# A^T W in three column parts, the first v chunk ahead of the weights, and softmax row sums as one more column of a product

## Chip, cores, metric

One core of one Trainium2 chip. The metric is the device time of one execution in microseconds (us). The span on a profile page is about 1.9 us shorter than the time of the same execution.

## The reference, cut to what matters

```python
# B, N, C = 4, 6144, 256; d_ff = 768; inputs float32
qn = q / (norm(q, axis=1) + 1e-6);  kn = k / (norm(k, axis=1) + 1e-6)
a = softmax(kn.transpose(0, 2, 1) @ qn / tau, -1)          # B x 256 x 256
x = (v @ a).reshape(B * N, C)
h = maximum(maximum(x @ w1, x @ w2), x @ w3)               # B*N x 768
out = h @ w_out                                            # B*N x 256
```

The kernel forms A^T W (`aw`, 256 x 768 for each of three weights) once per batch, and then runs 12 chunks of 512 rows of v through six h blocks each. It saves the product v A. The price is a short stage at each batch boundary: softmax, row sums, A^T W. Products land in tiles of PSUM; an eviction is the copy of such a tile to SBUF by ScalarE or VectorE, here with the scaling by 1/row sum, and frees the tile. The granted clock is the share of full speed that the profile shows for TensorE.

## The kernel before: what the change and the argument touch

```python
ps_h = tile_pool(name="ps_h", bufs=6, PSUM)   # h products, row sums and A^T W share six PSUM tiles
ps_x = tile_pool(name="ps_x", bufs=2, PSUM)
...
load_w(0)          # first halves (384 columns) of the three weights, software DMA queue
load_v(0)
load_w(1)          # second halves
load_v(1)
...                # w_out, load_v(2)

def rowsums(et):                                    # four one-column products
    ...
    DVE.reciprocal(out=rinv, in_=rs_ps[:, 0:CC])

def aw_half(et, rinv, aw, fh, at=(), between=None): # six groups: 3 weights x 2 row blocks
    for m in range(3):
        for ic in range(CC):
            ew = htile("ew_ps")
            for j in range(CC):
                PE.matmul(ew[:, :FH], lhsT=et[...], rhs=w_sb[m][:, j, fsl], ...)
            # evicted with scale=rinv, by ScalarE and VectorE in turn
...
def h_block(gi, aw, fc):                            # six products, then s_mx on ScalarE, two maxima on VectorE
    ...
et = softmax_t(*ps)
rinv = rowsums(et)
aw_half(et, rinv, aw, 0, [2], lambda: v_transpose_pe(0))  # v chunk 0 on TensorE
v_transpose(1)                                            # v chunk 1 by DMA transpose
for b in range(B):
    for ch in range(NCH):
        v_transpose(gi + 2)                               # DMA transpose, two chunks ahead
        if ch == 0:  gaps[0].append(lambda: aw_half(et, rinv, aw, 1))
        ...
        if more and ch == NCH - 1:                        # last chunk of a batch
            gaps[0]: norms; gaps[1]: exp_t; gaps[4]: rowsums
        for fc in range(FC):
            h_block(gi, aw, fc)
            for f in gaps[fc]: f()
        if more and ch == NCH - 1:
            aw_half(et, rinv, aw, 0)                      # behind the sixth h block
```

## Time and profile before

| | before |
|---|---|
| time, median | 586.5 us at first, 585.9 to 586.4 in the later sets |
| TensorE busy | 557.8 us, 95% of the span |
| TensorE waits for chunk 1's transpose | 5.0 us, once |
| twelve h products after that wait | 5.30 us (2.6 at the full clock), ending at 61.39 |
| first A^T W product to end of the second half, at a boundary | 5.30 us for 5.19 of work |

The prediction shows the lines of these. To read them: a wait counts only where it ends last.

### The profile page before, as it was taken

The numbers are of one execution on the slowest core, as the hardware profiler recorded it, in microseconds if no ns is written. First come the engines' busy times: TensorE is split into PE (matmuls) and PEld (weight loads), VectorE is DVE, ScalarE is ACT, GpSimd is POOL, SyncE is SP. The second block draws the span as 40 slices with busy tenths as digits, with TensorE's granted clock in tenths as the row PEclk, the third lists the DMA queues.
The fourth block names the chain that finished last, engine by engine and source line by source line (L and its number), as shares of the span: only waits on it lengthen the run. The fifth ranks groups of instructions, "written<-read, shape, count | busy, mean of one in ns | idle before, by whom it ended". The sixth has DMA issues, their size and how long they took to land.

```text
span 584.5 us, 9286 instructions
## 1 busy us (share of the span) xinstructions
PE 557.8 (95%) x3316; PEld 327.9 (56%) x3316; DVE 405.5 (69%) x623; ACT 305.6 (52%) x526; POOL 225.3 (39%) x232
## 2 busy tenths in 40 slices
PE   2786999999999999999999999999999999999997
PEld 2652555555575555555575555555575555555554
DVE  0035678778748787777848778777857777778775
ACT  0033357676735447767646446767745444444442
POOL 4241017877671006777770105777671000000000
PEclk9998899999999999999999999999999999999999
DMA  8999927988468635888649624899646344323211
GB/s 77 107 171 163 140 56 135 141 122 155 89 118 120 105 101 94 156 131 134 124 87 145 108 83 99 125 155 133 119 91 127 73 90 117 82 58 106 55 72 73
DMA packets 75134, 64.83 MB, mean 111 GB/s; under 512 B 52304, under 2 KB 61392, under 8 KB 75088
## 3 DMA queue, kind: packets, MB, share of 16 engines
q0 software_dynamic: 18400, 26.75, 38.8%
q1 hardware_dynamic: 56544, 37.23, 24.9%
q8 instruction: 26, 0.43, 0.3%
q10 hardware_dynamic: 144, 0.26, 0.1%
q14 instruction: 20, 0.16, 0.1%
HBM read 78.64 MB, written 25.17 MB: 178 GB/s over the span
## 4 chain that ended last, share of the span: by engine, by line
PE 90%; DMA 9%; POOL 1%; issue 0%; DVE 0%; POOLq 0%
PE h_ps L320 63%; PE o_ps L339 21%; DMA q_sb<-in_q_dram 3%; PE gram L226 3%; DMA vt_sb<-v_sb 2%; PE ew_ps L273 2%; DMA k_sb<-in_k_dram 2%; DMA v_sb<-in_v_dram 1%; PE o_ps L359 0%; POOL w_sb L128 0%; POOL k_sb L99 0%; PE n_ps L207 0%; PE n_ps L209 0%; DVE o_sb L365 0%; POOL ident masks.py:199 0%
## 5 line engine op out<-in xcount | busy, mean ns | idle before, releaser
L320 PE MATMUL h_ps<-vt_sb,aw_sb 128*128 128x512 bf16 x1728 | 409.0, 381 | 5.0 <-DMA vt_sb<-v_sb 5.0
L324 DVE TENSOR_TENSOR s_mx<-h_ps,s_mx 128x512 bf16<-128x512 f32 x288 | 197.8, 687 | 105.8 <-ACT s_mx L323 98.7
L320 PEld LDWEIGHTS <-aw_sb 128*128 128x128 bf16 x1728 | 168.8, 98 | 169.9 <-DMA vt_sb<-v_sb 5.5
L323 ACT ACTIVATE s_mx<-h_ps 128x512 bf16<-128x512 f32 x288 | 171.4, 595 | 138.8 <-PE h_ps L320 137.5
L325 DVE TENSOR_TENSOR ht_sb<-h_ps,s_mx 128x512 bf16<-128x512 f32 x288 | 199.3, 692 | 30.7 <-DVE s_mx L324 0.5
L195 POOL TENSOR_TENSOR acc<-acc,sq 128x768 f32<-128x768 f32 x90 | 147.5, 1650 | 70.8 <-ACT sq L189 70.6
L339 PE MATMUL o_ps<-wo_sb,ht_sb 128*128 128x256 bf16 x1128 | 154.0, 273 | 0.0
L339 PEld LDWEIGHTS <-ht_sb 128*128 128x128 bf16 x1128 | 110.5, 98 | 53.3 <-issue 0.6
L342 ACT ACTIVATE o_sb<-o_ps 128x512 f32<-128x512 f32 x94 | 56.1, 597 | 83.0 <-PE o_ps L339 83.0
L110 POOL DMA_DIRECT2D v_sb<-in_v_dram x48 | 26.7, 559 | 105.3 <-DMA vt_sb<-v_sb 101.6
L189 ACT ACTIVATE sq<-q_sb 128x768 bf16<-128x768 fp8e4 x48 | 40.5, 844 | 0.0
L189 ACT ACTIVATE sq<-k_sb 128x768 bf16<-128x768 fp8e4 x48 | 40.1, 835 | 0.0
L192 POOL CAST acc<-sq 128x768 f32<-128x768 bf16 x6 | 4.9, 820 | 74.7 <-ACT sq L189 74.7
L102 POOL DMA_DIRECT2D q_sb<-in_q_dram x32 | 17.6, 553 | 12.4 <-DMA k_sb<-in_k_dram 11.0
L157 PE MATMUL kk<-k_sb 128*128 128x256 fp8e4 x48 | 7.8, 339 | 13.6 <-DMA k_sb<-in_k_dram 13.6
L99 POOL DMA_DIRECT2D k_sb<-in_k_dram x31 | 17.0, 551 | 1.0 <-POOLq L439 0.8
L273 PE MATMUL ew_ps<-w_sb,et 128*128 128x384 bf16 x96 | 17.1, 326 | 0.0
L276 ACT ACTIVATE aw_sb<-ew_ps,rinv 128x384 bf16<-128x384 f32 x24 | 13.8, 581 | 6.1 <-PE ew_ps L273 5.1
L226 PE MATMUL gram<-k_sb,q_sb 128*128 128x512 fp8e4 x144 | 16.8, 276 | 0.0
L226 PEld LDWEIGHTS <-q_sb 128*128 128x256 fp8e4 x144 | 15.9, 136 | 0.6
L178 ACT ACTIVATE lnk<-kb_ps 128x256 f32<-128x256 f32 x1 | 0.4, 384 | 27.6 <-PE kb_ps L175 27.6
L157 PEld LDWEIGHTS <-k_sb 128*128 128x256 fp8e4 x48 | 6.5, 182 | 14.7 <-DMA k_sb<-in_k_dram 14.7
(49 smaller groups left out, 107.7 us busy)
## 6 DMA issues: line engine op xcount, KB each, us to landing
out_dram<-o_sb SPq DMA_DIRECT2D x47, 512.0 KB, 2.9
v_sb<-in_v_dram POOLq DMA_DIRECT2D x48, 256.0 KB, 4.0
k_sb<-in_k_dram POOLq DMA_DIRECT2D x24, 192.0 KB, 5.5
q_sb<-in_q_dram POOLq DMA_DIRECT2D x24, 192.0 KB, 7.0
k_sb<-in_k_dram POOLq DMA_DIRECT2D x5, 256.0 KB, 11.1
q_sb<-in_q_dram POOLq DMA_DIRECT2D x5, 256.0 KB, 19.4
w_sb<-in_moe_w_dram POOLq DMA_DIRECT2D x6, 192.0 KB, 8.9
vt_sb<-v_sb SPq DMA_TRANSPOSE x47, 3.7
```

The costliest lines, as they stand in the source:

```text
L102: POOL.dma_start(out=qk[b][0][:, g0:g0 + w, :], in_=q_r[b][:, g0:g0 + w, :])
L110: POOL.dma_start(out=t, in_=v_r[gi // NCH, gi % NCH])
L189: ACT.activation(out=sq, in_=src, func=AF.Square)
L195: POOL.tensor_tensor(out=acc, in0=acc, in1=sq, op=ALU.add)
L226: PE.matmul(g[:, j * C:(j + 1) * C], lhsT=qt[:, tsl, j * P:(j + 1) * P], rhs=kt[:, tsl, :], start=(tp == 0 and j == 0), stop=(tp == NG // ...
L273: PE.matmul(ew[:, :FH], lhsT=et[:, j, ic * P:(ic + 1) * P], rhs=w_sb[m][:, j, fsl], start=(j == 0), stop=(j == CC - 1))
L320: PE.matmul(t.rearrange("p (t n) -> p t n", t=TPC), lhsT=aw[m][:, ic, fsl], rhs=vt[:, :, ic, :], start=(ic == 0), stop=(ic == CC - 1))
L323: ACT.activation(out=s_mx, in_=hp[0], func=AF.Copy)
L324: DVE.tensor_tensor(out=s_mx, in0=hp[1], in1=s_mx, op=ALU.max)
L325: DVE.tensor_tensor(out=ht[:, fc, :], in0=hp[2], in1=s_mx, op=ALU.max)
L339: PE.matmul(st["ps"][:, half], lhsT=ht[:, fc, t * P:(t + 1) * P], rhs=wo_sb[:, fc, :], start=(fc == 0), stop=(fc == FC - 1))
L342: ACT.activation(out=st["o"][:, t - 1:t + 1, :].rearrange("p t d -> p (t d)"), in_=st["ps"], func=AF.Copy)
```

## The change

The intent: let v chunk 0 and its transposes run while the softmax finishes, start the h blocks after a third of A^T W instead of a half, and save the row-sum products.

```diff
-    load_w(0)
-    load_v(0)
-    load_w(1)
+    FW = 2 * P;  FN = d_ff // FW;  PADW = FW + 4
+    w_sb = [consts.tile([P, FN, CC, PADW], BF16, ...) for i in range(3)]   # was [P, CC, d_ff]
+    load_v(0)
+    load_w(0)          # thirds of 256 columns, 512 B rows at 520 B steps
+    load_w(1)
+    load_w(2)
     load_v(1)
...
-    DVE.memset(ones_c, 1.0)
+    DVE.memset(w_sb[0][:, 0, :, FW:PADW], 1.0)
...
-    def rowsums(et): ...
-    def aw_half(et, rinv, aw, fh, ...):
+    def aw_part(et, rinv, aw, fp):
         for m in range(3):
+            cols = FW + 1 if (fp == 0 and m == 0) else FW
             for ic in range(CC):
...
+                if cols > FW:
+                    DVE.reciprocal(out=rinv[:, ic:ic + 1], in_=ew[:, FW:cols])
...
-    rinv = rowsums(et)
-    aw_half(et, rinv, aw, 0, [2], lambda: v_transpose_pe(0))
+    v_transpose_pe(0)
+    aw_part(et, rinv, aw, 0)
...
-                gaps[0].append(lambda: aw_half(et, rinv, aw, 1))
+                for fp in range(1, FN):
+                    gaps[2 * fp - 2].append(lambda fp=fp: aw_part(et, rinv, aw, fp))
...
-                gaps[4].append(lambda: st.update(r=rowsums(st["e"])))
```

(The boundary's call becomes `aw_part(et, rinv, aw, 0)` in the same place.)

More of the change, by code (lines that the diff above doesn't have):

```diff
@@ L61 @@
     NCH = N // CHUNK
-    FH = d_ff // 2
     q_r = q.rearrange("b (p g) c -> b p g c", p=P)
@@ L121, with load_w @@
                 make_identity(nc, ident)
-    w_sb = [consts.tile([P, CC, d_ff], BF16, name=f"w{i}_sb") for i in range(3)]
-    def load_w(fh):
-        fsl = slice(fh * FH, (fh + 1) * FH)
+    FW = 2 * P
+    FN = d_ff // FW
+    PADW = FW + 4
+    w_sb = [consts.tile([P, FN, CC, PADW], BF16, name=f"w{i}_sb") for i in range(3)]
+    def load_w(fp):
+        fsl = slice(fp * FW, (fp + 1) * FW)
         for wt, w in zip(w_sb, w_list):
-            POOL.dma_start(out=wt[:, :, fsl], in_=w.rearrange("(cc p) f -> p cc f", p=P)[:, :, fsl])
+            POOL.dma_start(out=wt[:, fp, :, 0:FW], in_=w.rearrange("(cc p) f -> p cc f", p=P)[:, :, fsl])
+    load_v(0)
     load_w(0)
-    load_v(0)
     load_w(1)
+    load_w(2)
     load_v(1)
@@ L140 @@
     DVE.memset(ones_f, 1.0)
-    ones_c = consts.tile([P, 1], BF16, name="ones_c")
-    DVE.memset(ones_c, 1.0)
+    DVE.memset(w_sb[0][:, 0, :, FW:PADW], 1.0)
     warm = consts.tile([P, CHUNK], BF16, name="warm")
@@ L254, in alloc_aw @@
         return [aw_pool.tile([P, CC, d_ff], BF16, name=f"aw{m}_sb", tag=f"aw{m}") for m in range(3)]
-    def rowsums(et):
-        rinv = sm.tile([P, CC], FP32, name="rinv")
-        rs_ps = htile("rs_ps")
-        for ic in range(CC):
-            for j in range(CC):
-                PE.matmul(rs_ps[:, ic:ic + 1], lhsT=et[:, j, ic * P:(ic + 1) * P], rhs=ones_c,
-                          start=(ic == 0 and j == 0), stop=(j == CC - 1), skip_group_check=True)
-        DVE.reciprocal(out=rinv, in_=rs_ps[:, 0:CC])
-        return rinv
-    def aw_half(et, rinv, aw, fh, at=(), between=None):
-        fsl = slice(fh * FH, (fh + 1) * FH)
+    def aw_part(et, rinv, aw, fp):
+        fsl = slice(fp * FW, (fp + 1) * FW)
         n = 0
         for m in range(3):
+            cols = FW + 1 if (fp == 0 and m == 0) else FW
             for ic in range(CC):
@@ L272, in aw_half @@
                 for j in range(CC):
-                    PE.matmul(ew[:, :FH], lhsT=et[:, j, ic * P:(ic + 1) * P], rhs=w_sb[m][:, j, fsl],
+                    PE.matmul(ew[:, :cols], lhsT=et[:, j, ic * P:(ic + 1) * P], rhs=w_sb[m][:, fp, j, 0:cols],
                               start=(j == 0), stop=(j == CC - 1))
+                if cols > FW:
+                    DVE.reciprocal(out=rinv[:, ic:ic + 1], in_=ew[:, FW:cols])
                 if n % 2 == 0:
-                    ACT.activation(out=aw[m][:, ic, fsl], in_=ew[:, :FH], func=AF.Copy,
+                    ACT.activation(out=aw[m][:, ic, fsl], in_=ew[:, :FW], func=AF.Copy,
                                    scale=rinv[:, ic:ic + 1])
                 else:
-                    DVE.tensor_scalar_mul(out=aw[m][:, ic, fsl], in0=ew[:, :FH],
+                    DVE.tensor_scalar_mul(out=aw[m][:, ic, fsl], in0=ew[:, :FW],
                                           scalar1=rinv[:, ic:ic + 1])
                 n += 1
-                if n in at:
-                    between()
     vts = {}
@@ L375 @@
     aw = alloc_aw()
-    rinv = rowsums(et)
-    aw_half(et, rinv, aw, 0, [2], lambda: v_transpose_pe(0))
+    rinv = sm.tile([P, CC], FP32, name="rinv")
+    v_transpose_pe(0)
+    aw_part(et, rinv, aw, 0)
     v_transpose(1)
@@ L417 @@
             if more and ch == NCH - 1:
-                et, rinv = st["e"], st["r"]
+                et = st["e"]
+                rinv = sm.tile([P, CC], FP32, name="rinv")
                 aw = alloc_aw()
-                aw_half(et, rinv, aw, 0)
+                aw_part(et, rinv, aw, 0)
     o_last(B * NCH - 1)
```

## The prediction

> **What bounds the kernel now.** I read the page first: busy shares, then the slices, then the chain of waits that ended last.
>
> ```profile
> span 584.5 us, 9286 instructions
> PE 557.8 (95%) x3316; PEld 327.9 (56%) x3316; DVE 405.5 (69%) x623; ACT 305.6 (52%) x526; POOL 225.3 (39%) x232
> ...
> PEclk9998899999999999999999999999999999999999
> ...
> PE 90%; DMA 9%; POOL 1%; issue 0%; DVE 0%; POOLq 0%
> ```
>
> TensorE carries 90% of the chain and the DMA 9%, so two things can move the time: TensorE work or TensorE stalls anywhere after the start, and the transfers of the start. Then I asked for TensorE's own waits (engine line, waited for, us in total, times, longest):
>
> ```profile
> PE kk L157 <- DMA k_sb<-in_k_dram: 13.6, 7, 5.2
> PE h_ps L320 <- DMA vt_sb<-v_sb: 5.0, 1, 5.0
> PE gram L169 <- DMA q_sb<-in_q_dram: 3.2, 3, 1.6
> PE vt_ps L305 <- DMA v_sb<-in_v_dram: 0.5, 1, 0.5
> PE rs_ps L261 <- ACT et L237: 0.2, 1, 0.2
> ```
>
> The change aims at the last two, 0.7 us in all. The second is the important one: one stall of 5.0 us. The chain in order of time, from 30 to 60 us, shows which work it hangs on (start, us, what):
>
> ```profile
> 12.99 20.07 DMA q_sb<-in_q_dram
> 33.06 0.29 issue
> 33.35 0.70 POOL w_sb L128
> 34.05 0.09 issue
> 34.14 1.40 POOL w_sb L128 x2
> 35.54 8.08 DMA v_sb<-in_v_dram
> 43.62 0.02 issue
> 43.63 12.41 DMA vt_sb<-v_sb
> 56.05 0.05 issue
> 56.09 4.02 PE h_ps L320 x9
> ```
>
> The q load, then v chunk 1 landing at 43.62, then its DMA transpose landing at 56.05. The softmax and the first A^T W products (38.2 to 44.5 us) are not on this chain: TensorE finishes chunk 0 at about 51.1 and waits for the transposed chunk 1 until 56.09. After that stall TensorE never waits for a DMA; its limit is its own pace.
>
> **What the Trainium skill says.** "TensorE: Matmul & The Clock Gate", Back-to-back issue gap: warm gap N/2.4 + 2.5 ns, so 216 ns for 512 columns, 162 for 384, 109 for 256. The trace agrees: six h products span 1.29 us (215 each), six output products of 256 columns 0.66 us (110), twelve A^T W products of 384 columns 1.95 us (179.18 to 181.13; 162 each). Part 1 of that page says that a window of about 3.4 us without work halves the clock until a busy window has passed. The trace agrees: the granted clock is 0.50 from 55 to 61 us, and the twelve h products after the stall take 5.30 us instead of 2.6. "DMA: Bandwidth & Descriptors", Queues, rings and completion order, says that each DMA engine takes turns between queues by packets, and Why small descriptors are slow, that each packet carries a fixed cost. The trace agrees with both: between 47.3 and 53.3 us the software queue moved 479 packets and the transpose queue 466, one for one; and 512 B packets pass more slowly per byte than 768 B ones (worked out below).
>
> **Start: v chunk 0 ahead of the weights.** This removes the 0.5 us wait at the TensorE transposes of v, which now run while the exponentials finish. It also makes the first part smaller: 1.30 us of products instead of 1.95 before the first h block, plus smaller evictions. I estimate that the first h block starts near 39.8 instead of 41.2 us and that chunk 0 ends about 1 us earlier, near 50. But chunk 1's transpose does not come earlier. The order of the software queue is unchanged from v chunk 1 on, and the bytes ahead of it are the same: chunk 0 and all of w. Only their cutting changes: 6 loads x 256 packets of 768 B become 9 x 256 of 512 B. Costs from the DMA view: in 34.2 to 36.2 us, w alone, 553 packets of which 34 are tiny, 519 in 2.0 us, so 16 engines give 62 ns each; in 42.3 to 43.5 us, almost all 512 B rows of w_out, 423 in 1.2 us, 45 ns each. Before 1536 x 62/16 = 5.9 us, after 2304 x 45/16 = 6.5 us: +0.6, and three more completions, say +0.7. Each software load waits for the one eight places before it, but about seven stay in flight, several us of transfers, so the queue doesn't run dry although three loads are added.
>
> When chunk 1 has landed the backlog is the same as before: w_out, v chunks 2 to 5, one k and one q piece. The 1024 packets of the transpose go one for one with it and finish about 1.7 us after it is drained (pure transposes reach about 1000 packets per us). So the transpose lands at 56.05 + 0.7 = 56.8. **The stall grows from 5.0 to about 6.5 us and swallows the whole gain at the front; the start costs +0.7.** The cold-clock stretch stays. Its length depends on where in its window work resumes, so I give it 0 +/- 0.7 us.
>
> **The three later batch boundaries.** These lie on TensorE's path with no slack behind them. Before (TensorE, start, us, xcount):
>
> ```profile
> 177.84 0.19 PE L261 MATMUL rs_ps<-ones_c,et 128*128 128x1 bf16 x2
> 177.89 1.46 PE L320 MATMUL h_ps<-vt_sb,aw_sb 128*128 128x512 bf16 x6
> 179.18 2.11 PE L273 MATMUL ew_ps<-w_sb,et 128*128 128x384 bf16 x12
> 181.13 1.56 PE L320 MATMUL h_ps<-vt_sb,aw_sb 128*128 128x512 bf16 x6
> 182.53 2.11 PE L273 MATMUL ew_ps<-w_sb,et 128*128 128x384 bf16 x12
> 184.48 0.81 PE L320 MATMUL h_ps<-vt_sb,aw_sb 128*128 128x512 bf16 x3
> ```
>
> From 179.18 to 184.48, 5.30 us, against 5.19 of work at the warm pace (1.95 + 1.29 + 1.95): only 0.11 lost. Twelve products of 1.95 us cover the time that VectorE needs to finish the last block's two maxima and to scale its share.
>
> *Removed:* four row-sum products, 0.10 us of TensorE (177.79 to 177.89), and their reciprocal. *Total product work:* 2 x 1.95 against 3 x 1.30, the same; the 257th column in four products is nothing (4 x 0.4 ns). *Moved:* the reciprocals now stand in VectorE's order behind the maxima of the last h block, so no eviction starts before they end. With t = 0 at the first A^T W product (179.18 before): the second maximum began at 179.98 and releases VectorE at 180.59, t = 1.4; two short reciprocals and their hand-over to t = 1.6; ScalarE's first eviction, about 0.47 us for 256 columns (0.58 for 384), ends near t = 2.1. The later ones follow at 0.43 (VectorE: 1.66/3 = 0.55 for 384 columns, less 128/0.96 GHz). The last product of the h block can then start at t = 3.0, and the block ends near 3.4. Before, the same block ended at 182.53, t = 3.35, with 1.95 us of product work done; now only 1.30 is done by then. **Loss 0.65, after taking off the 0.10.**
>
> *Second part, after the first h block:* six tiles of PSUM rotate. The sixth product group of the part needs the tile of that block's third h product, which VectorE frees at the end of its second maximum (184.03 to 184.1 before, t = 4.9). With 384 columns the sixth group came 5 x 0.325 = 1.63 us after the part's start, 184.16, just in time. With 256 it comes 1.08 us after, so it waits about 0.5. *Third part, after the third h block:* the same, about 0.4, since the block's maxima end some 1.4 us after the block and the sixth group comes after 1.1.
>
> Sum per boundary 0.65 + 0.5 + 0.4 = 1.55; three boundaries 4.65. The first batch has the same waits, but they are covered by the stall on chunk 1. All of it: +0.7 + 4.65 = +5.3 on 586.51, 591.8. I take 591.2, because the waits by tiles may partly be absorbed (each delay of TensorE lets VectorE catch up for the next).
>
> **Rivals.** (1) *The front gain is real*: if chunk 1's transpose came earlier by the about 1 us that chunk 0 gains, the time would be 585 to 586. For it: the chain's first 33 us are load-bound, and the order of v and w was the thing changed. Against: no byte ahead of chunk 1 disappears. (2) *The boundaries are neutral*: VectorE is 69% busy overall and could drain in time; then only +0.7 remains minus 0.3 for the row sums, 587. Against: already before, the h block at 181.13 took 1.40 instead of 1.29, so no slack is there. (3) *The w rows, now placed at 520 B steps, are slow to write or the padded tile disturbs the loads*: at 60 ns per packet the weights would take 8.6 us, +2.7 instead of +0.6, giving 593 to 594. Nothing in the trace of before shows such a step, so I can't exclude it. (4) *The stall shrinks enough to keep the clock warm*: gain 2.7 us from the clock and up to 5 from the stall, about 579. The transpose would have to land some 2 us or more earlier, and nothing moves it so.
>
> **Range and chances.** Rivals 1 and 2 set the low end, 586.5 (small chance of 585); the full sum with rival 3 sets the high end, 594.5. Two per cent is 11.7 us: neither the largest loss that I can add up (about 8) nor rival 4's gain reaches it. So within 2%: 0.97; slower 0.02; faster 0.01.
>
> **What would show it.** Right: chunk 1's transpose lands between 56.5 and 57.2, TensorE's wait for it is over 6 us, the first h block starts before 40.3; at each boundary six products groups of the second part last about 1.8 us instead of 1.3, and TensorE loses 1.2 to 1.8 us from the first product to the end of the third part. Wrong at the front: the transpose lands before 56. Wrong at the boundaries: each part lasts 1.3 us and the h block after the first one ends by t = 2.7. The forecast as a whole is wrong if the time is under 586.5 or above 594.5.

## The result, and the profile after

The changed kernel took 588.73 us (median of 4) beside 586.0 for the kernel before. The ratio is 1.0051, 95% interval 1.0029 to 1.0073. A second set on another occasion gave 587.90 beside 586.38, ratio 1.0031 (1.0019 to 1.0044). A ratio is the mean time of one kernel's fast runs over that of the other's in the same rounds, so it is not quite the ratio of the medians. By these ratios the change costs 1.8 to 3.0 us, under 2%.

What TensorE waited for in the changed kernel (us in total, times, longest):

```profile
PE h_ps L314 <- DMA vt_sb<-v_sb: 6.8, 1, 6.8
PE h_ps L314 <- ACT aw_sb L272: 1.0, 4, 0.4
PE ew_ps L267 <- DVE ht_sb L319: 0.9, 3, 0.3
```

The two waits that the change aimed at (for v chunk 0 and for the exponentials) are gone. The wait for chunk 1 has grown from 5.0 to 6.8, and two new waits stand in and behind the first part of a batch. The chain in order of time:

```profile
38.56 5.79 DMA v_sb<-in_v_dram
44.36 13.14 DMA vt_sb<-v_sb
57.55 4.87 PE h_ps L314 x11
```

The same two transfers end the start as before, and they end later: 57.51 against 56.05. (This view ends at 62 us; all twelve products took 5.26, to 62.81.) This profile was taken of the slowest of the four runs; in a second profile, below, the transpose lands 1.2 us earlier. A boundary on TensorE (start, us, products):

```profile
180.40 1.26 PE L267 MATMUL ew_ps<-w_sb,et 128*128 128x257 bf16 x10
181.97 0.38 PE L267 MATMUL ew_ps<-w_sb,et 128*128 128x256 bf16 x2 [0.31 <-DVE ht_sb L319]
182.56 1.47 PE L314 MATMUL h_ps<-vt_sb,aw_sb 128*128 128x512 bf16 x6 [0.21 <-ACT aw_sb L272]
183.86 1.47 PE L267 MATMUL ew_ps<-w_sb,et 128*128 128x256 bf16 x12
185.24 1.46 PE L314 MATMUL h_ps<-vt_sb,aw_sb 128*128 128x512 bf16 x6
...
188.48 1.47 PE L267 MATMUL ew_ps<-w_sb,et 128*128 128x256 bf16 x12
189.79 0.82 PE L333 MATMUL o_ps<-wo_sb,ht_sb 128*128 128x256 bf16 x6
```

Read the starts. The first part needs 1.30 us of work but holds TensorE from 180.40 to 182.56, 2.16 us. The h block after it then runs at full pace (1.30). The second part takes 1.38 and the third 1.31. Over pure work that is 0.86 + 0.08 + 0.01 = 0.95 us. The kernel before lost 0.11 there and spent 0.10 on row sums, so the change costs 0.74 us per boundary and 2.2 us for three. VectorE at the same place shows what TensorE waits for:

```profile
181.23 0.69 DVE L319 TENSOR_TENSOR ht_sb<-h_ps,s_mx 128x512 bf16<-128x512 f32 x1
181.84 0.22 DVE L270 RECIPROCAL rinv<-ew_ps 128x1 f32<-128x1 f32 x2
182.03 0.84 ACT L272 ACTIVATE aw_sb<-ew_ps,rinv 128x256 bf16<-128x256 f32 x2 [1.64 <-DVE rinv L270]
```

The reciprocals stand behind the last block's second maximum, and ScalarE sits idle for 1.64 us until the first of them.

### The profile page after: what moved, and what is told of

Same layout as the page of the kernel before. It is cut to its first block, busy times and chain, and to the rows that moved or that the text cites. A ratio compares the mean times of both kernels' runs of the same rounds, so it can differ in the third digit from the quotient of the medians.

```text
span 588.0 us, 9376 instructions
## 1 busy us (share of the span) xinstructions
PE 558.6 (95%) x3348; PEld 333.2 (57%) x3348; DVE 407.3 (69%) x639; ACT 307.2 (52%) x538; POOL 227.5 (39%) x235
## 4 chain that ended last, share of the span: by engine, by line
PE 89%; DMA 8%; POOL 1%; DVE 1%; issue 0%; ACT 0%; POOLq 0%
PE h_ps L314 63%; PE o_ps L333 21%; DMA v_sb<-in_v_dram 3%; DMA q_sb<-in_q_dram 3%; PE gram L229 3%; DMA vt_sb<-v_sb 2%; PE ew_ps L267 2%; POOL k_sb L98 1%; PE o_ps L353 0%; DVE ht_sb L319 0%; ACT aw_sb L272 0%; POOL w_sb L131 0%; PE n_ps L210 0%; PE n_ps L212 0%; DVE o_sb L359 0%
## 5 line engine op out<-in xcount | busy, mean ns | idle before, releaser
L192 ACT ACTIVATE sq<-q_sb 128x768 bf16<-128x768 fp8e4 x48 | 40.5, 845 | 0.0
L272 ACT ACTIVATE aw_sb<-ew_ps,rinv 128x256 bf16<-128x256 f32 x36 | 15.6, 473 | 9.4 <-DVE rinv L270 5.5
L267 PE MATMUL ew_ps<-w_sb,et 128*128 128x256 bf16 (+1 forms) x144 | 18.2, 272 | 0.9 <-DVE ht_sb L319 0.9
L267 PEld LDWEIGHTS <-et 128*128 128x128 bf16 x144 | 14.0, 98 | 5.4 <-issue 1.5
L275 DVE TENSOR_SCALAR aw_sb<-ew_ps,rinv 128x256 bf16<-128x256 f32 x36 | 15.1, 477 | 0.1
```

What stands on the lines that cost most here:

```text
L192: ACT.activation(out=sq, in_=src, func=AF.Square)
L267: PE.matmul(ew[:, :cols], lhsT=et[:, j, ic * P:(ic + 1) * P], rhs=w_sb[m][:, fp, j, 0:cols], start=(j == 0), stop=(j == CC - 1))
```

## The experiments

Before their measurements, my theories were: (A) the start hangs on chunk 1's DMA transpose, so a gain ahead of it is swallowed; (B) a boundary loses because evictions start late, behind the reciprocals; (C) the wait for chunk 1 and the halved clock after it are what the start costs. Rivals stand in each expectation. There were twelve runs, the last of them the changed kernel again; all gave correct results. Times are medians; the kernel before was timed beside each set (585.86, 585.90 and 586.38 us).

| kernel | time | ratio to before (95%) |
|---|---|---|
| v_first | 585.62 | 0.9999 (0.9987 to 1.0011) |
| sum_col | 587.43 | 1.0020 (1.0007 to 1.0033) |
| parts_sep | 587.55 | 1.0029 (1.0017 to 1.0042) |
| w_thirds | 585.81 | 0.9997 (0.9985 to 1.0009) |
| after_aligned | 588.26 | 1.0046 (1.0032 to 1.0060) |
| before_v1pe | 579.54 | 0.9895 (0.9881 to 0.9908) |
| vfirst_v1pe | 578.59 | 0.9872 (0.9856 to 0.9888) |
| after_v1pe | 580.60 | 0.9912 (0.9898 to 0.9925) |
| after_early | 588.52 | 1.0039 (1.0026 to 1.0051) |
| after_v1pe_early | 580.32 | 0.9896 (0.9881 to 0.9911) |
| vfirst_v1pe_early | 578.35 | 0.9863 (0.9850 to 0.9877) |
| after_again | 587.90 | 1.0031 (1.0019 to 1.0044) |

**v_first: one part alone, v chunk 0 ahead.**

```diff
-    load_w(0)
     load_v(0)
+    load_w(0)
     load_w(1)
...
+    v_transpose_pe(0)
     rinv = rowsums(et)
-    aw_half(et, rinv, aw, 0, [2], lambda: v_transpose_pe(0))
+    aw_half(et, rinv, aw, 0)
```

> The kernel before with one part of the change: v chunk 0 loaded ahead of the weights and transposed before the row sums. Theory A (the start hangs on the transpose of v chunk 1, and only the packets of w move it): chunk 1 lands at 43.6 +- 0.3 us and its transpose at 56.1 +- 0.4, as in the kernel before; TensorE's wait for it grows by what chunk 0 gains, to between 5.0 and 6.5 us; boundaries unchanged at 5.30 us from the first A^T W product to the end of the second half; time within 0.5 us of the kernel before. Rival (the front gain counts): 1 us or more faster.

Measured: ratio 0.9999. Chunk 0's first h block started at 40.26 instead of 41.23 us, 0.97 earlier, and TensorE's wait for chunk 1 grew:

```profile
PE h_ps L320 <- DMA vt_sb<-v_sb: 6.4, 1, 6.4
```

Boundaries took 5.31 us. Theory A holds: TensorE starts chunk 0 earlier, the wait behind it grows, and the time does not change.

**sum_col: one part alone, the sum column, in halves.**

```diff
-    w_sb = [consts.tile([P, CC, d_ff], ...)]
+    w_sb = [consts.tile([P, 2, CC, FH + 4], ...)]     # ones in the last columns of w_sb[0]
...
+            cols = FH + 1 if (fh == 0 and m == 0) else FH
+                if cols > FH:
+                    DVE.reciprocal(out=rinv[:, ic:ic + 1], in_=ew[:, FH:cols])
...
-                gaps[4].append(lambda: st.update(r=rowsums(st["e"])))
```

> The kernel before with one part: row sums as one more column of the first product, still in two halves, w loaded in 768 B rows. Theory B (the boundary loss comes from the reciprocals standing behind the maxima AND from 1.3 us of products being too short a cover): with halves the products take 1.95 us and cover most of the 2.16 us until the first eviction is done, so about +0.1 to +0.2 us per boundary, +0.3 to +0.6 in all, start unchanged (transpose at 56.1 +- 0.4). Rival (the reciprocal's place alone makes the loss of 0.75 us per boundary): +2.2 us.

Measured: a boundary took 5.62 us instead of 5.30; less the 0.10 of saved row sums that is +0.22, 0.66 in three. The longer halves cover most of the delay. The mean span of its runs is 0.7 us above that of the kernel before, which fits. The time is 1.2 us above it, more than the 0.3 to 0.6 expected, since time minus span is 2.4 us here and 1.9 in the kernel before; what happens in that half microsecond outside the span stays open.

**parts_sep: the changed kernel with separate row sums.**

```diff
-            cols = FW + 1 if (fp == 0 and m == 0) else FW
+            cols = FW
+    # rowsums() as in the kernel before: at the start after v_transpose_pe(0), and in gaps[4]
```

> The changed kernel with one part undone: separate row-sum products in the fifth gap, as before, still three parts and v first. Theory B: the reciprocal no longer delays the first eviction; from the first product to the end of the second part 4.3 us instead of 4.84, so per boundary about +0.3 us against the kernel before instead of +0.75, 1.0 to 1.4 us faster than the changed kernel in all; the start keeps its +0.7 to +1.5 us; +1.7 to +2.4 us against the kernel before. Rival (three parts alone make the loss): as slow as the changed kernel, +2.7 to +3.

Measured: +1.7 us on the kernel before. The changed kernel's two ratios give +3.0 and +1.8, so the time alone does not tell whether this is faster; the boundary does. There the three parts alone still cost something:

```profile
179.76 1.47 PE L278 MATMUL ew_ps<-w_sb,et 128*128 128x256 bf16 x12
181.14 0.38 PE L325 MATMUL h_ps<-vt_sb,aw_sb 128*128 128x512 bf16 x1
181.70 1.25 PE L325 MATMUL h_ps<-vt_sb,aw_sb 128*128 128x512 bf16 x5 [0.18 <-DVE aw_sb L286]
182.79 1.47 PE L278 MATMUL ew_ps<-w_sb,et 128*128 128x256 bf16 x12
184.17 1.46 PE L325 MATMUL h_ps<-vt_sb,aw_sb 128*128 128x512 bf16 x6
```

From 179.76 to 184.17 it took 4.41 us instead of 4.84. Over pure work, the third part included, 0.53 are lost against 0.11 before: +0.4 per boundary. So of 0.74 about 0.4 comes from the shorter part and the rest from the sum column, whose reciprocals stand behind the maxima. Both halves of theory B are needed, as sum_col says from the other side.

**w_thirds: the kernel before with w in nine pieces of 512 B rows.**

```diff
-    def load_w(fh): fsl = slice(fh * FH, (fh + 1) * FH)
+    def load_w(fp): fsl = slice(fp * 256, (fp + 1) * 256)
     load_w(0)
-    load_v(0)
     load_w(1)
+    load_v(0)
+    load_w(2)
```

> The kernel before with w loaded in nine pieces of 256 columns (512 B rows, dense tile) instead of six of 384 (768 B), v chunk 0 after the sixth; products in halves as before. Theory A: only the packet size moves v chunk 1: it lands at 44.2 +- 0.3 us instead of 43.6, its transpose at 56.7 to 57.5; chunk 0 starts some 1 to 2 us later, hidden in the wait for chunk 1; boundaries unchanged at 5.30; time +0.6 to +1.5 us. Rival (the padded 520 B step slows the loads of the changed kernel): chunk 1 at 43.6 to 43.8 here, time within 0.3 us.

Measured: chunk 1 landed at 43.60 us and its transpose at 56.25, almost as in the kernel before (43.62, 56.05), and the time was equal. Theory A's figures for this run missed, and the rival's came true: the small packets cost much less than the sum had it. The rival's cause, the padding, was tested next. A second thing shows here: the wait for chunk 1 was shorter (4.3 us, since chunk 0 began later), the clock was still full from 56 to 57 us (half in the kernel before), and the twelve products after the wait took 4.29 us instead of 5.30.

**after_aligned: rows of w at 1024 B steps.**

```diff
-    PADW = FW + 4
+    PADW = 2 * FW
```

> The changed kernel with one number altered: rows of w at 1024 B steps instead of 520 B, so that each 512 B row starts on a multiple of 512 B; everything else as changed. Theory A2, formed from the dense 512 B loads that did not delay chunk 1 (43.60 us): the 520 B step makes the rows slower to land; chunk 1 lands at 43.6 to 43.9 us instead of 44.1 to 44.4, its transpose at 56.2 to 56.7 instead of 57.1 to 57.5; 0.5 to 1 us faster than the changed kernel, +1.7 to +2.3 us against the kernel before. Rival (three more loads and their completions, or v chunk 0 in front, delay chunk 1): no difference from the changed kernel, chunk 1 at 44.1 to 44.4.

Measured: 1.0046 to the kernel before, between the changed kernel's two results (1.0051, 1.0031); chunk 1 at 43.90 us, its transpose at 56.59, inside what the changed kernel itself shows in two profiles (43.82 to 44.36, 56.31 to 57.51). It was not faster, as theory A2 had it. The step of 520 B is not shown to matter, and two profiles of one kernel differ by more than the effect sought.

**before_v1pe: v chunk 1 on TensorE.**

```diff
-    v_transpose(1)
...
+            if gi == 0:
+                gaps[3].append(lambda: v_transpose_pe(1))
```

> The kernel before with v chunk 1 transposed on TensorE after the fourth h block of chunk 0, instead of by DMA. Theory C (the wait for that transpose, and the halved clock after it, are what the start costs): TensorE's wait of 5.0 us goes, the clock stays at 1.00 from 54 to 64 us (another 2.6 us), TensorE does 0.5 to 0.7 us more; chunk 2's transpose, by DMA, lands before it is needed at about 63 us; 6.5 to 7.5 us faster than the kernel before, 578.5 to 579.5. Rival (the wait only moves to chunk 2's transpose): a wait of 2 us or more on chunk 2, gain under 4 us.

Measured: 6.2 us faster by the ratio (6.4 by the medians), a little less than the 6.5 to 7.5 expected. No wait of TensorE for a transposed chunk is left, and the clock stays up where it was halved (columns: TensorE's busy time, weight loads, VectorE, ScalarE, POOL, granted clock, DMA share, GB/s). First the kernel before:

```profile
56.00:58.00 2.00, 1.91 (x5) 0.74 (x6) 0.00 (x0) 0.60 (x1) 1.43 (x3) 0.50 0.96 194
```

Then with chunk 1 on TensorE:

```profile
56.00:58.00 2.00, 2.00 (x14) 1.22 (x13) 1.79 (x3) 1.08 (x3) 1.46 (x3) 1.00 0.36 54
```

Theory C holds: 14 products run in these two microseconds in place of 5 (six of the 14 are the smaller output products), and the wait did not move to chunk 2.

**vfirst_v1pe: v chunk 0 first, and chunk 1 on TensorE** (the edits of v_first and before_v1pe together).

> The kernel before with v chunk 0 loaded first and v chunk 1 transposed on TensorE. Theory A and C: with the wait for chunk 1 gone, the front gain of v first (chunk 0 starts 0.97 us earlier) now counts: 0.7 to 1.1 us faster than the kernel before with v chunk 1 on TensorE alone. Rival (the front gain is worth nothing for another reason): the same time as that one.

Measured: 578.59 against 579.54, 0.95 us faster by the medians and 1.2 by the means; in the two profiles chunk 0's first h block starts 0.74 us earlier. That the medians differ by almost the 0.97 us of v_first is partly luck, since this kernel's four runs span 1.3 us. With the wait behind it gone, the front gain counts, at about its size.

**after_v1pe: the changed kernel with chunk 1 on TensorE** (the edit of before_v1pe).

> The changed kernel with v chunk 1 transposed on TensorE. Theory: the start no longer depends on when chunk 1's DMA transpose lands, so what is left against the kernel before with v chunk 1 on TensorE is the boundary loss of 3 x 0.75 = 2.25 us minus the front gain of 0.3 to 1.1 us: 1.1 to 2.0 us slower than that one, and 2.2 to 3 us slower than v first with v chunk 1 on TensorE. Rival (the loss of the change lies in the start): no slower than the kernel before with v chunk 1 on TensorE.

Measured: 580.60, 1.06 above before_v1pe and 2.0 above vfirst_v1pe (2.2 by means), just under what was expected. No DMA transpose ends the start here, and this difference agrees with the boundaries' 2.2 us by themselves.

**after_early: the first part behind the fifth h block.**

```diff
+                def first_part():
+                    st.update(r=sm.tile([P, CC], FP32, name="rinv"), aw=alloc_aw())
+                    aw_part(st["e"], st["r"], st["aw"], 0)
+                gaps[4].append(first_part)
...
-                aw_part(et, rinv, aw, 0)       # behind the sixth h block
```

> The changed kernel with the first column part of the next batch moved from behind the sixth h block of a batch's last chunk to behind its fifth, so that the sixth h block covers the reciprocals and evictions. Theory B (the loss at a boundary is TensorE waiting for evictions that start only after the reciprocals behind the maxima, with nothing to do meanwhile): the 0.85 us per boundary go, no wait of TensorE for aw or for a PSUM tile is left, 2.3 to 2.9 us faster than the changed kernel, 0 to +0.8 us against the kernel before. Rival (three parts cost TensorE time of themselves, in weight loads or issue): under 1 us faster than the changed kernel.

Measured: 588.52, no faster. The wait was not covered; it moved along:

```profile
177.79 1.26 PE L267 MATMUL ew_ps<-w_sb,et 128*128 128x257 bf16 x10
179.27 0.38 PE L267 MATMUL ew_ps<-w_sb,et 128*128 128x256 bf16 x2 [0.22 <-DVE ht_sb L319]
179.86 2.75 PE L314 MATMUL h_ps<-vt_sb,aw_sb 128*128 128x512 bf16 x12 [0.20 <-ACT aw_sb L272]
```

The first part again held TensorE for 2.07 us. The h block that follows it here works with the *old* batch's `aw` and needs no datum of the part, yet it waited for ScalarE's eviction. What it waited for is a PSUM tile. In the built program the part's six groups take all six tiles of the pool (banks 0, 4, 3, 2, 5, 1 at this boundary), and the next h product gets bank 0, the tile of the part's first group, which is free only after reciprocal and eviction. So theory B as I stated it falls in one point. Late evictions do cost the time, but here through the tiles that they hold, and moving the part did not help, since it takes the whole pool. A pool with more tiles could not be tried: with six tiles here and two in the other pool no PSUM is left, and with seven here the program does not build. A part that takes fewer tiles was not tried.

**after_v1pe_early and vfirst_v1pe_early: both cures together** (the edits above; in the second one with halves and separate row sums).

> The changed kernel with both cures: v chunk 1 on TensorE, and the first part one block earlier. Theories B and C together, adding up: 2.3 to 2.9 us faster than with v chunk 1 on TensorE alone (580.6), 577.7 to 578.3 us. Rival (the two overlap): under 1.5 us faster than that one.

> The kernel before with v chunk 0 first, v chunk 1 on TensorE, halves and separate row sums, and the first half one block earlier. The halves lose only 0.11 us per boundary, so about 0.3 us faster than without the last step (578.6), 578.0 to 578.5 us; within 0.5 us of the changed kernel with both cures. Rival (an earlier half crowds VectorE and ScalarE at the end of the chunk): slower than 578.6 us.

Measured: 580.32 against 580.60 without the move, and 578.35 against 578.59. The first misses its expectation for the reason just shown. The second lies inside it, but its profile gives no reason: its halves held TensorE for 2.13 and 2.11 us instead of 1.95 each, and the mean spans of the two kernels are equal (576.6 and 576.5), so I count it as the same. Either vfirst kernel beats both the kernel before and the changed one, by 1.3 to 1.4% and, by the quotients of the ratios, 1.6 to 1.9%.

**after_again: the changed kernel once more.**

> The changed kernel once more, without an edit, for a second profile of its start and a time on the same chip as its variants. Boundaries as in its first profile, 4.84 us from the first product to the end of the second part and 1.31 for the third; chunk 1's transpose between 56.5 and 57.6 us, below the 57.51 of the first profile if that one, the slowest of four runs, was an extreme; +2.5 to +3.2 us against the kernel before.

Measured: 587.90, +1.8 us by the ratio, below the +2.5 to +3.2 expected. Boundaries as in the first profile (4.86 us, and 1.31). The start is not (chain in order of time):

```profile
43.82 12.49 DMA vt_sb<-v_sb
56.36 4.51 PE h_ps L314 x12
```

The transpose landed at 56.31, 1.2 us earlier than in the first profile of the same kernel. The instant scatters by more than the effect sought. Over the five profiles with thirds and v first (57.51, 56.31, 57.03, 56.59, 56.56) the mean is 56.80; over the three with halves and 768 B rows (56.05, 56.48, 56.09) it is 56.21. So the transpose lands about 0.6 us later, with that scatter on it.

That is not yet a cost in time, since the twelve products behind the wait differ too. They took 5.30 us in all three profiles with halves and 4.06 to 5.26 in the five with thirds (mean 4.74), so they ended at 61.55 and at 61.59 on average (61.39 to 61.82, and 60.69 to 62.81). The granted clock makes the difference. In the nine profiles in which a DMA transpose ends the start, read in windows of 0.1 us, it fell to one half 2.1 to 5.4 us after the last product before the wait, and stayed there for 6.8 us in seven of them and for 3.4 us in two (after_aligned, w_thirds). No run shows that the change decides which. So a cost of the start in time is not shown; a single profile can be 1.4 us later (the first) or 0.7 earlier (after_aligned) than the kernel before.

## Why the prediction was right, and which terms were mis-sized

The time lay in the predicted range, and the mechanism is as predicted at the start and for the first part of a boundary. For the second and third part it is not. The centre (+5.3 summed, 591.2 taken) was too high by more than 2 us, and that one step carries most of it. Of the signs that the prediction named, the first h block before 40.3 came true (40.08 and 40.26 in the two profiles); the landing missed its 56.5 to 57.2 on either side (57.51 and 56.31), and the wait was over 6 us in only one of them (6.8 and 5.4); a second part of 1.8 us and a loss of 1.2 to 1.8 us per boundary did not come (1.38 and 0.95).

**The start's gain is swallowed: right.** v_first shows it alone (0.97 us earlier, wait 6.4, time equal), and vfirst_v1pe shows the gain reappear when the wait is taken away. That the predicted landing of 56.8 is the mean of five profiles is partly luck: the +0.7 rested on +0.6 for the packets of w, which measured +0.2, and what makes the rest of the 0.6 us stays open. The +0.7 us of cost in time is not shown, since on average the products behind the wait ended no later (61.59 against 61.55).

**The packets of w, +0.6: too large.** The DMA view of a stretch in which w alone moves, in the changed kernel (36.5 to 40.5 us) and, as the prediction used it, in the kernel before (34.2 to 36.2):

```profile
DMA packets 1602, 0.77 MB, mean 193 GB/s; under 512 B 95, under 2 KB 1602, under 8 KB 1602
```

```profile
DMA packets 553, 0.40 MB, mean 198 GB/s; under 512 B 34, under 2 KB 553, under 8 KB 553
```

That is 1507 rows of 512 B in 4.0 us, 42 ns each on 16 engines, where I had taken 45 from a stretch that also held larger packets. All of w then takes 2304 x 42.5/16 = 6.1 us against 1536 x 61.7/16 = 5.9: +0.2. w_thirds agrees.

**The first part at a boundary, loss 0.65: right in size.** First product to end of the first h block was 3.46 us (3.4 predicted) against 3.35 before, with 0.65 of work less done and 0.10 saved: 0.66. Its cause was only half named: I wrote of evictions and their `aw` data, and after_early shows that the PSUM tile alone is enough to make the wait.

**The second and third part, 0.5 + 0.4: the step that failed.** The prediction had the sixth group of such a part wait for the tile of the h block's third product, taking it that the six tiles rotate. They don't rotate in a fixed order. In the built program the sixth group of these parts gets the tile of the same part's first group (banks 0, 4, 3, 2, 5, 0 in one boundary's second part), which ScalarE has freed by then. The trace agrees: the second part ends at 185.24, when the second maximum, which I had it wait for, still runs (184.62 to 185.31). Measured 0.08 and 0.01 in place of 0.5 and 0.4, 0.8 us per boundary and 2.4 in all, the size of the miss. Only the *first* part has the wait that I described (0.31 us for `ht_sb`). There the built program does give the sixth group the tile of the last block's third h product (bank 3 at this boundary), in sum_col too; with separate row sums, in the kernel before and in parts_sep, the sixth group gets the part's own first tile. So the sum column goes with it; why the build chooses so is not shown.

**The sum with measured terms:** 3 x 0.74 = 2.2 us at the boundaries and on average nothing that shows at the start, beside 3.0 and 1.8 us by the two ratios. Profile by profile it fits better. In the first, the twelve products ended 1.42 us later than in the kernel before, with 2.2 that is 3.6, and the span was 3.5 us longer; in the second they ended 0.52 earlier, which gives 1.7, and the span was 1.6 longer.

**The rivals.** (1) and (2) fall: neither is the front gain felt nor are the boundaries neutral. (3) falls by its own figure, 42 ns per packet in place of 60, and after_aligned shows no difference either. (4), a start that keeps the clock warm, was ruled out rightly for this change. It is what before_v1pe then brought about by other means, worth 6.2 us, more than the change was about.

## What to carry to other kernels

Before shortening work that ends in a wait, ask what ends the wait: here 1 us gained ahead of a DMA transpose was worth nothing until that transpose was moved to TensorE, and then about 1 us. A stage cut into smaller pieces gives TensorE less to do while the pieces are evicted; with one shared PSUM pool a late eviction can hold up the next block even where that block needs none of its data (0.20 us in after_early). Where a wait lets the clock fall, compare the instant at which the slow stretch ends, not the one at which the wait does. Read the tile that an instruction really gets from the built program; don't assume that a pool rotates.

## What the Trainium skill lacked or had wrong

- "DMA: Bandwidth & Descriptors", Queues, rings and completion order, tells of the turns that queues take by packets, but gives no time for a transfer that shares the engines so. Here two queues moved 479 and 466 packets in the same 6.0 us, and a DMA transpose issued beside a backlog of loads took 12.4 to 13.1 us to land, against a median of 3.7 us over the run.
- The same page, Why small descriptors are slow, works its fixed cost per packet out for 256 B only. Here rows of 768 B took 61.7 ns and rows of 512 B took 42.5 ns, 12.4 and 12.1 B/ns, so the smaller rows cost 3% per byte. Its How a descriptor splits into AXI transactions tells of reads that start off a multiple of 256 B, and not of writes; rows written at 520 B steps and at 1024 B steps gave no difference that the runs could tell (1.0051 and 1.0031 against 1.0046).
- "TensorE: Matmul & The Clock Gate", Part 1, has the clock halved after an idle window of about 3.4 us. Here it fell as early as 2.1 us after the last product (after_again) and as late as 5.4 us (w_thirds, 1.1 us after work had begun again), and stayed halved for 3.4 us in two profiles and for 6.8 us in seven. The twelve products behind the wait, 2.6 us at the full clock, took 4.06 to 5.30 us.
- No page says how a tile pool picks the PSUM bank. Here the six tiles were not given out in a fixed order: the sixth group of a part got the tile of the part's own first group or that of the h block before it, and this went with no wait or one of 0.31 us.
